# Column-tiled float32 numerators and denominators for all head pairs of a linear attention, and a lag of two units in the ELU layer behind it

## The chip, the core and the metric

The kernel runs on one core of a Trainium2 chip. Its engines are TensorE (PE in the profile; PEld is its weight load), VectorE (DVE), ScalarE (ACT), GpSimd (POOL) and SyncE (SP), which here only issues DMAs. Each engine works through its own instructions strictly in order; they wait for one another through semaphores. The metric is the device time of one launch in microseconds (us). A difference of under 0.5%, about 7 us, is taken as no change.

## The reference

```python
def phi(x):                                     # x: one head, 576 x 64
    proj = x @ w_phi                            # 128 features
    proj = proj - max(abs(proj), axis=-1)
    return concatenate([exp(proj), exp(-proj)]) # 256 features
q_p, k_p = phi(q), phi(k)                       # 4 batches x 8 heads
kv  = k_p.T @ v
num = q_p @ kv
den = q_p @ sum(k_p) + 1e-6
x   = num / den                                 # -> 2304 tokens x 512

x   = elu(x @ w_in) @ w_out                     # 512 -> 2048 -> 512
p   = domain_probs / sum(domain_probs)
out = sum over 4 experts of p[:, e] * (relu(x @ w1[e]) @ w2[e])   # 512 -> 1024 -> 512
```

All is float32.

## The kernel before, in words

**Stages.** Attention works on 16 pairs of heads; a pair fills 128 partitions (2 heads of 64). The ELU layer works on 9 token tiles of 256 tokens and, of its 2048 hidden features, on 4 units of 256 each for the first half (class `Elu`). The second half of the hidden features and the four experts follow in the classes `UpElu`, `Up`, `Out` and `Down`. Attention pairs 0 to 3 (the first batch) run alone, because every token tile needs all heads of a batch. Then the other pairs are fed in between the ELU products. In the same time the weights, which arrive as 64-bit floats, are converted by ScalarE, VectorE and GpSimd (`convert64`): 32 conversions for the first half of the hidden features, 32 for the second, whose VectorE work is held back (`hold`).

**Number forms.** Most products are done as three fp32r products of split operands, high x high, high x low and low x high, so an operand exists as `...h` and `...l`. Plain float32 products, which TensorE does in two passes (two matmul records each), are used in attention's projections, its keys-values product, and in the numerators of pairs 0 to 6 (`wide`, below `NF32`).

**One pair** (`pair`, a generator that yields between its steps). Projections (L192, each head on 64 of the array's 128 rows) -> `guard` on VectorE (L198, L199) -> exponentials of the keys (L202, L203) -> keys times values (L231, L232) into `kvw` (L280); queries transposed (L238) and their exponentials `ew` (L251), or `eh` and `el` (L256, L261) in the split form. The values' tile has columns of ones beside the 64 columns of values, so one product of 128 columns gives numerators in one half of the partitions and the denominator, repeated, in the other. `num` (L303) does that for each half of the 576 tokens: 4 float32 products, or 12 split ones, into two PSUM banks, copied to `nd` by ScalarE (L313). One row of `nd` goes by DMA to `dn`, laid out over 128 partitions (L320), VectorE adds 1e-6 and inverts (L323, L324), SyncE stores the reciprocals to DRAM (`rec`, L325) and loads them back broadcast over 64 partitions (`rb`, L329). VectorE multiplies (L334, once for each head), and `put_x` makes the high part on ScalarE (L295) and the low part on GpSimd (L298).

**One ELU unit** (`Elu`). `l1`: 24 products (L499 to L501) into one bank, then ScalarE (L507, L508), VectorE (L510), ScalarE's `gh` (L511) and `gl` (L512, VectorE or GpSimd). `l2`: 24 products with `gh` and `gl` (L528 to L530) into the tile's two accumulator banks. `drive` calls `l1` of a unit and then `l2` of the unit `LAG` before it. Between them `slot` advances attention (RATE steps a slot) and the weights (WRATE, WSLOW or WFAST steps).

**What sets the order.** The code gives each engine's instructions in the order of its loops; a scheduler then moves instructions on each engine by its own estimate of time and by priorities. In the first stage two steps of the weights' generator follow each step of attention (PRE). The pool for `gh` and `gl` has LAG + 1 buffers.

## Time and profile before

| | us |
|---|---|
| three timed runs, median | 1417.93 |
| lowest and highest | 1412.84, 1418.87 |
| the profiled execution | 1418.54 |
| its span, first to last instruction | 1416.7 |
| TensorE matmul busy in it | 1367.7 |
| VectorE, ScalarE, GpSimd busy | 692.8, 629.8, 418.6 |

The profile is of one execution. A line of its groups gives the source line, the engine, the operation, output<-inputs with shapes, the count, the busy time and mean of one, and then the idle time of the engine just before those instructions with what ended most of it. A matmul's modelled duration includes its way through the array, so consecutive matmuls overlap; how fast they follow one another is read from their start times. A row of the table of stretches has, for each engine, the busy time and the number of instructions, then the granted share of TensorE's 2.4 GHz clock.

### The profile page before, as it was taken

How to read it: one execution, taken by the hardware profiler on the slowest of the kernel's cores; microseconds unless marked ns; L12 is line 12 of the kernel's file. 1: busy time of each engine (PE TensorE's matmuls, PEld its weight loads, DVE VectorE, ACT ScalarE, POOL GpSimd, SP SyncE). 2: the span in 40 equal slices, each digit the busy share in tenths (PEclk: the TensorE clock that was granted, in tenths of full speed). 3: DMA queues.
4: the chain of work that ended last, by engine and by line, in shares of the span. 5: the costliest groups of instructions: out<-in, count | busy, mean ns of one | idle time of the engine just before them, and what ended most of it. 6: DMA issues, size and time to landing. Idle time of an engine off the chain costs nothing.

```text
span 1416.7 us, 21809 instructions
## 1 busy us (share of the span) xinstructions
PE 1367.7 (97%) x8224; PEld 1262.2 (89%) x8224; DVE 692.8 (49%) x1233; ACT 629.8 (44%) x1417; POOL 418.6 (30%) x487
## 2 busy tenths in 40 slices
PE   6779999999999999999999999999999999999998
PEld 5669999999989899999898979888898989889897
DVE  6786566666564566684423423224433325323232
ACT  6676676666556646573333442122431214321121
POOL 5567465454446211263202440002420004300000
PEclk9999999999999999999999999999999999999999
DMA  5453343433323230346425143434146351433521
GB/s 176 137 159 118 115 147 94 131 114 112 103 82 127 56 118 29 127 164 208 148 98 205 38 137 109 156 111 149 50 145 210 102 178 46 141 119 127 179 67 67
DMA packets 105786, 173.46 MB, mean 122 GB/s; under 512 B 33488, under 2 KB 51024, under 8 KB 105680
## 3 DMA queue, kind: packets, MB, share of 16 engines
q1 hardware_dynamic: 98224, 162.55, 35.3%
q10 hardware_dynamic: 7456, 9.52, 1.9%
q8 instruction: 65, 1.06, 0.3%
q14 instruction: 41, 0.34, 0.1%
HBM read 118.13 MB, written 53.81 MB: 121 GB/s over the span
## 4 chain that ended last, share of the span: by engine, by line
PE 75%; DMA 7%; issue 4%; DVE 4%; POOL 4%; ACT 3%; SPq 1%; ACTq 0%; DVEq 0%; POOLq 0%
PE bank L619 10%; PE bank L620 10%; PE bank L621 10%; PE bank L721 9%; PE bank L722 9%; PE bank L723 9%; PE bank L698 2%; PE bank L699 2%; PE bank L700 2%; PE bank L231 2%; PE bank L311 2%; PE bank L528 1%; PE bank L499 1%; PE bank L529 1%; PE bank L530 1%
## 5 line engine op out<-in xcount | busy, mean ns | idle before, releaser
L620 PE MATMUL bank<-xv,w 128*128 128x384 f32 x840 | 282.4, 336 | 0.0
L619 PE MATMUL bank<-xv,w 128*128 128x384 f32 x840 | 279.3, 337 | 2.5 <-DVE c L670 1.9
L621 PE MATMUL bank<-xv,w 128*128 128x384 f32 x840 | 278.2, 336 | 0.0
L721 PE MATMUL bank<-w,h 128*128 128x512 f32 x576 | 226.3, 396 | 2.3 <-ACT h L635 2.3
L722 PE MATMUL bank<-w,h 128*128 128x512 f32 x576 | 228.0, 396 | 0.0
L723 PE MATMUL bank<-w,h 128*128 128x512 f32 x576 | 202.8, 396 | 0.0
L461 POOL TENSOR_TENSOR w<-wst,w 128x256 fp32r<-128x256 f32 x100 | 78.0, 798 | 363.1 <-ACT w L460 220.4
L619 PEld LDWEIGHTS bank<-xv,w 128*128 128x128 f32 x840 | 158.2, 188 | 11.0 <-DVE c L670 2.2
L620 PEld LDWEIGHTS bank<-xv,w 128*128 128x128 f32 x840 | 158.3, 188 | 4.8
L621 PEld LDWEIGHTS bank<-xv,w 128*128 128x128 f32 x840 | 157.8, 188 | 0.0
L636 DVE SCALAR_TENSOR_TENSOR h<-bank,h 128x384 fp32r<-128x384 f32 x144 | 77.2, 554 | 125.9 <-ACT h L635 125.9
L635 ACT ACTIVATE h<-bank 128x384 fp32r<-128x384 f32 x144 | 66.8, 489 | 151.7 <-PE bank L621 95.4
L721 PEld LDWEIGHTS bank<-w,h 128*128 128x128 f32 x576 | 108.4, 188 | 25.4 <-ACT h L635 3.3
L722 PEld LDWEIGHTS bank<-w,h 128*128 128x128 f32 x576 | 108.5, 188 | 23.1
L723 PEld LDWEIGHTS bank<-w,h 128*128 128x128 f32 x576 | 107.2, 188 | 21.8 <-DVE h L636 1.0
L625 ACT ACTIVATE cmab<-bank 128x384 f32<-128x384 f32 x60 | 29.4, 491 | 192.5 <-PE bank L621 192.5
L570 POOL TENSOR_TENSOR xv<-xs,xv 128x768 fp32r<-128x768 f32 x24 | 47.7, 1988 | 190.3 <-ACT xv L569 181.5
L528 PE MATMUL bank<-gh,w 128*128 128x256 f32 x288 | 82.6, 295 | 6.7 <-ACT gh L511 6.7
L633 DVE TENSOR_TENSOR c<-cmab,bank 128x384 f32<-128x384 f32 x48 | 26.6, 554 | 120.3 <-ACT cmab L625 120.3
L499 PE MATMUL bank<-xh,w 128*128 128x256 f32 x288 | 83.8, 292 | 1.6 <-ACT eh L256 1.6
L633 DVE TENSOR_TENSOR bank<-cm,bank 128x384 f32<-128x384 f32 x48 | 26.9, 561 | 116.6 <-PE bank L621 101.1
L529 PE MATMUL bank<-gl,w 128*128 128x256 f32 x288 | 81.0, 283 | 1.7 <-DVE gl L512 1.7
(117 smaller groups left out, 2840.5 us busy)
## 6 DMA issues: line engine op xcount, KB each, us to landing
xv<-xvd SPq DMA_DIRECT2D x42, 768.0 KB, 4.4
wst<-in_w SPq DMA_DIRECT2D x64, 256.0 KB, 2.8
xvd<-xv SPq DMA_DIRECT2D x21, 768.0 KB, 4.0
yscr<-y SPq DMA_DIRECT2D x54, 256.0 KB, 2.2
y<-yscr SPq DMA_DIRECT2D x54, 256.0 KB, 3.2
w<-in_w_in SPq DMA_DIRECT2D x32, 256.0 KB, 3.4
w<-in_w_out SPq DMA_DIRECT2D x32, 256.0 KB, 3.3
kq<-in_kq SPq DMA_DIRECT2D x16, 320.0 KB, 3.6
```

Of the source, the lines that this page charges most:

```text
L461: on[WL[v % len(WL)]].tensor_tensor(out=lo, in0=x, in1=f32(hi), op=ALU.subtract)
L499: PE.matmul(ph[:, j], w[:, 0, c], xh[:, kc], start=(kc == 0), stop=False)
L528: PE.matmul(o, w[:, 0, c], self.gh[:, j], start=start, stop=False)
L529: PE.matmul(o, w[:, 0, c], self.gl[:, j], start=False, stop=False)
L619: PE.matmul(o, hi[:, c], x[:, 0, kc], start=not more and kc == 0, stop=False, skip_group_check=more)
L620: PE.matmul(o, hi[:, c], x[:, 1, kc], start=False, stop=False, skip_group_check=more)
L621: PE.matmul(o, lo[:, c], x[:, 0, kc], start=False, stop=kc == 1, skip_group_check=more)
L635: A.activation(h[:, 0], c, ACTF.Relu)
L636: V.scalar_tensor_tensor(out=h[:, 1], in0=c, scalar=0.0, in1=f32(h[:, 0]), op0=ALU.max, op1=ALU.subtract)
L721: PE.matmul(self.acc, h[:, 0, c], w[:, 0], start=f == 0, stop=False)
L722: PE.matmul(self.acc, h[:, 0, c], w[:, 1], start=False, stop=False)
L723: PE.matmul(self.acc, h[:, 1, c], w[:, 0], start=False, stop=f == 2 * NQ - 1)
```

## The change

All 16 pairs take the plain float32 form; the split form and its tiles go. The numerators of a pair's two heads are computed as products of 64 columns each (the stationary operand is only the 64 columns of values), head 0 to partitions 0 to 63 and head 1 to partitions 64 to 127 of one bank. The denominators come from products of their own, of 32 columns of ones each: four groups of 32 partitions hold the two heads and the two halves of the tokens. These are computed first, copied to `dd`, and sent to `dn` by one DMA of four rows. The pair has one step (one `yield`) less. The copy to `nd` is one for each half, and the multiplication is one over 128 partitions. `LAG` goes from 1 to 2.

```diff
-LAG = 1
+LAG = 2
...
-        def split(ef, c0, n):
-            for h in range(0 if wide else 2):
-                G.tensor_tensor(out=el[:, h, :, c0:c0 + n], in0=ef[:, h], in1=f32(eh[:, h, :, c0:c0 + n]), op=ALU.subtract)
...
-        A.activation(kvw if wide else kvh, pk, ACTF.Copy)
-        yield
-        if not wide:
-            V.tensor_tensor(out=kvl, in0=pk, in1=f32(kvh), op=ALU.subtract)
-        split(ef1, 256, 256)
-        split(efm, 512, D)
+        A.activation(kvw, pk, ACTF.Copy)
         yield
...
-        nd = [a1.tile([P, S], F32, tag=f"nd{h}", name=f"nd{h}", bufs=2) for h in range(2)]
+        nd = a1.tile([P, S], F32, tag="nd", name="nd", bufs=2)
...
         def num(s):
-            sl = slice(s * HS, (s + 1) * HS)
-            pn = [bank() for _ in range(2)]
-            terms = ((kvw, ew),) if wide else ((kvh, eh), (kvh, el), (kvl, eh))
-            last = 2 * len(terms) - 1
-            for h in range(2):
-                for k in range(last + 1):
-                    c, (w, m) = k // len(terms), terms[k % len(terms)]
-                    PE.matmul(pn[h][:, :HS], w[:, 2 * h + c], m[:, h, c, sl], start=(k == 0), stop=(k == last))
-            for h in range(2):
-                A.activation(nd[h][:, sl], pn[h][:, :HS], ACTF.Copy)
-
+            pn = bank()
+            for c in range(2):
+                for h in range(2):
+                    r = slice(h * D, h * D + D)
+                    PE.matmul(pn[r, :HS], kvw[:, 2 * h + c, r], ew[:, h, c, half(s)], start=(c == 0), stop=(c == 1))
+            A.activation(nd[:, half(s)], pn[:, :HS], ACTF.Copy)
+
+        def den():
+            pd = bank()
+            for c in range(2):
+                for h in range(2):
+                    for s in range(2):
+                        g = (2 * h + s) * Q
+                        ones = D - h * D
+                        PE.matmul(pd[g:g + Q, :HS], kvw[:, 2 * h + c, ones:ones + Q], ew[:, h, c, half(s)], start=(c == 0), stop=(c == 1))
+            A.activation(dd, pd[:, :HS], ACTF.Copy)
+
+        dd = a1.tile([P, HS], F32, tag="dd", name="dd")
+        den()
+        dn = a1.tile([P, S // D], F32, tag="dn", name="dn")
+        A.dma_start(dn, dd[::Q].rearrange("g (a b) -> g a b", b=S // D))
+        yield
         num(0)
-        yield
         num(1)
-        dn = a1.tile([P, S // D], F32, tag="dn", name="dn")
-        for h in range(2):
-            A.dma_start(dn[h * D:h * D + D], nd[h][D - h * D:D - h * D + 1, :].rearrange("o (a b) -> o a b", b=S // D))
         yield
...
-        for h in range(2):
-            r = slice(h * D, h * D + D)
-            with tc.issue_after(mark[0]):
-                V.tensor_tensor(out=xf[r], in0=nd[h][r], in1=rb[r], op=ALU.mult)
+        with tc.issue_after(mark[0]):
+            V.tensor_tensor(out=xf, in0=nd, in1=rb, op=ALU.mult)
```

The changed file is 19 lines shorter, so a line such as L499 is L480 in it. In the order of instructions, products that the code issues are counted, so a float32 product is one row and two records of the trace.

TensorE in the first stage, from the keys-values products of the second pair to the first transpose of the third. Before:

```order
L232 MATMUL bank<-vt_186,kpm 128x128
L192 MATMUL bank<-wbd,kq 128x128 x8
L311 MATMUL bank<-ew,kvw 128x288 x4
L192 MATMUL bank<-wbd,kq 128x128 x8
L311 MATMUL bank<-ew,kvw 128x288 x4
L238 MATMUL bank<-ident,qd_496 128x128
```

and now (L294 is `den`, L284 is `num`, L190 the projections):

```order
L230 MATMUL bank<-vt_186,kpm 128x128
L190 MATMUL bank<-wbd,kq 128x128 x8
L294 MATMUL bank<-ew,kvw 32x288 x8
L284 MATMUL bank<-ew,kvw 64x288 x8
L190 MATMUL bank<-wbd,kq 128x128 x8
L236 MATMUL bank<-ident,qd_504 128x128
```

The last numerators stood behind the second group of projections; now denominators and numerators stand ahead of it.

TensorE among the ELU products, at the numerators of the sixth pair. Before:

```order
L500 MATMUL bank<-xl,w 128x256
L501 MATMUL bank<-xh,w 128x256
L311 MATMUL bank<-ew,kvw 128x288 x4
L499 MATMUL bank<-xh,w 128x256
L500 MATMUL bank<-xl,w 128x256
```

and now, at the denominators of the same pair (L480 to L482 are the first layer's products, L509 to L511 the second layer's):

```order
L481 MATMUL bank<-xl,w 128x256
L482 MATMUL bank<-xh,w 128x256
L294 MATMUL bank<-ew,kvw 32x288 x8
L509 MATMUL bank<-gh,w 128x256
L510 MATMUL bank<-gl,w 128x256
L511 MATMUL bank<-gh,w 128x256
```

Untiled products had untiled ones on both sides; the denominators, and 12 rows later the numerators, are tiled ones among untiled.

TensorE at a change from the first to the second layer's products, after attention has ended. Before:

```order
L501 MATMUL bank<-xh,w 128x256
L528 MATMUL bank<-gh,w 128x256 x2
L499 MATMUL bank<-xh,w 128x256
L500 MATMUL bank<-xl,w 128x256
L501 MATMUL bank<-xh,w 128x256
L529 MATMUL bank<-gl,w 128x256
L530 MATMUL bank<-gh,w 128x256
L528 MATMUL bank<-gh,w 128x256
```

and now:

```order
L480 MATMUL bank<-xh,w 128x256
L481 MATMUL bank<-xl,w 128x256
L482 MATMUL bank<-xh,w 128x256
L509 MATMUL bank<-gh,w 128x256
L510 MATMUL bank<-gl,w 128x256
L511 MATMUL bank<-gh,w 128x256
```

The scheduler had put first-layer products between the two that need `gh` alone and the first that needs `gl`; now 24 and 24 stand in plain blocks.

## Rows read from the trace of the kernel before

**Rows 1.** The page's first part: busy time, share of the span, instructions.

```profile
PE 1367.7 (97%) x8224; PEld 1262.2 (89%) x8224; DVE 692.8 (49%) x1233; ACT 629.8 (44%) x1417; POOL 418.6 (30%) x487
```

**Rows 2.** Busy time in stretches: stretch, length, each engine, clock, DMA share, GB/s.

```profile
0.00:88.80 88.80, 64.77 (x502) 55.76 (x502) 65.79 (x150) 57.70 (x153) 48.69 (x77) 0.96 0.53 155
88.80:106.30 17.50, 11.84 (x82) 10.20 (x80) 14.94 (x30) 12.89 (x34) 11.12 (x17) 1.00 0.53 166
106.30:386.00 279.70, 276.75 (x2290) 266.49 (x2290) 176.53 (x348) 181.41 (x436) 151.82 (x191) 0.99 0.38 114
...
473.00:1416.70 943.70, 933.67 (x4747) 851.44 (x4746) 389.46 (x645) 328.63 (x701) 164.96 (x164) 1.00 0.36 122
...
107.00:111.00 4.00, 4.00 (x24) 4.00 (x23) 3.25 (x7) 3.31 (x8) 3.43 (x5) 0.57 0.01 4
```

**Rows 3.** TensorE's groups of the ELU products, and one piece of its timeline.

```profile
L499 PE MATMUL bank<-xh,w 128*128 128x256 f32 x288 | 83.8, 292 | 1.6 <-ACT eh L256 1.6
L528 PE MATMUL bank<-gh,w 128*128 128x256 f32 x288 | 82.6, 295 | 6.7 <-ACT gh L511 6.7
L529 PE MATMUL bank<-gl,w 128*128 128x256 f32 x288 | 81.0, 283 | 1.7 <-DVE gl L512 1.7
...
106.34 0.50 PE L528 MATMUL bank<-gh,w 128*128 128x256 f32 x2 [3.91 <-ACT gh L511]
```

**Rows 4.** Timeline of TensorE at one half's wide numerators: start, us, what.

```profile
125.42 2.10 PE L311 MATMUL bank<-ew,kvw 128*128 128x288 f32 x8
127.15 0.50 PE L499 MATMUL bank<-xh,w 128*128 128x256 f32 x1
127.48 0.28 PE L500 MATMUL bank<-xl,w 128*128 128x256 f32 x1
```

**Rows 5.** Timeline of TensorE at one half's split numerators, first record and next line.

```profile
219.94 0.29 PE L311 MATMUL bank<-eh,kvh 128*128 128x288 f32 x1
...
221.53 0.28 PE L528 MATMUL bank<-gh,w 128*128 128x256 f32 x1
```

**Rows 6.** Timeline of TensorE: full height, a start of half height, a whole visit.

```profile
20.75 1.06 PE L231 MATMUL bank<-vt,kp 128*128 128x128 f32 x8
...
23.07 0.38 PE L192 MATMUL bank<-wbd,kq 64*128 64x128 f32 x2
...
146.34 0.28 PE L530 MATMUL bank<-gh,w 128*128 128x256 f32 x1
146.55 1.16 PE L192 MATMUL bank<-wbd,kq 64*128 64x128 f32 x16
147.64 0.39 PE L528 MATMUL bank<-gh,w 128*128 128x256 f32 x1
147.87 0.28 PE L529 MATMUL bank<-gl,w 128*128 128x256 f32 x1
```

**Rows 7.** The start up to 107 us: GpSimd, VectorE's groups, waits, SyncE's timeline.

```profile
97.98 1.75 POOL L298 TENSOR_TENSOR xl<-xf,xh 128x256 fp32r<-128x256 f32 x3
...
L334 DVE TENSOR_TENSOR xf<-nd,rb 64x576 f32<-64x576 f32 x8 | 7.4, 919 | 0.1
L116 DVE TENSOR_SCALAR pcs<-pcs 128x256 f32<-128x256 f32 x26 | 11.2, 430 | 11.6 <-ACT pcs L112 11.5
...
SPq L325 <- DMA dn<-nd: 15.2, 4, 8.1
...
59.98 0.42 SPq L148 DMA_DIRECT2D kq<-in_kq  x1
69.31 0.33 SPq L325 DMA_DIRECT2D rec<-dn  x1
```

**Rows 8.** Timeline of VectorE and TensorE at the end of the ELU layer.

```profile
469.79 0.42 DVE L448 TENSOR_TENSOR wtmp<-wst 128x256 f32<-128x256 f32 x1
...
469.93 0.69 PE L619 MATMUL bank<-xv,w 128*128 128x384 f32 x1 [1.90 <-DVE c L670]
```

More of the change, by code (lines that the diff above doesn't have):

```diff
@@ L23 @@
 HS = S // 2
+Q = 32
 TS = 256
@@ L55 @@
 PB = 4
-NF32 = 7
 LDB = 1
@@ L183, in pair @@
         kt, qt = kq[:, :512], kq[:, 640:]
-        wide = i < NF32
         def proj(src):
@@ L239, in tpose @@
             return pt
-        if wide:
-            ew = a1.tile([P, 2, 2, S], F32, tag=("eh", "el")[i % 2], name="ew")
-        else:
-            eh = a1.tile([P, 2, 2, S], F32R, tag="eh", name="eh")
-            el = a1.tile([P, 2, 2, S], F32R, tag="el", name="el")
+        ew = a1.tile([P, 2, 2, S], F32, tag=("eh", "el")[i % 2], name="ew")
         def qexp(ps, c0, n):
             src = ps[:, :512].rearrange("p (h s) -> p h s", h=2)[:, :, :n] if n > P else blocks(ps, 2)[:, :, P - n:]
-            if wide:
-                for c, sc in ((0, 1.0), (1, -1.0)):
-                    A.activation(ew[:, :, c, c0:c0 + n], src, ACTF.Exp, scale=sc)
-                return None
-            ef = a1.tile([P, 2, 2, n], F32, tag=f"ef{n}", name="ef")
-            for dst in (ef, eh[:, :, :, c0:c0 + n]):
-                for c, sc in ((0, 1.0), (1, -1.0)):
-                    A.activation(dst[:, :, c], src, ACTF.Exp, scale=sc)
-            return ef
-        def split(ef, c0, n):
-            for h in range(0 if wide else 2):
-                G.tensor_tensor(out=el[:, h, :, c0:c0 + n], in0=ef[:, h], in1=f32(eh[:, h, :, c0:c0 + n]), op=ALU.subtract)
-        if wide:
-            kvw = a1.tile([P, 4, P], F32, tag=("kvh", "kvl")[i % 2], name="kvw")
-        else:
-            kvh = a1.tile([P, 4, P], F32R, tag="kvh", name="kvh")
-            kvl = a1.tile([P, 4, P], F32R, tag="kvl", name="kvl")
-        ef0 = qexp(tpose(0), 0, 256)
+            for c, sc in ((0, 1.0), (1, -1.0)):
+                A.activation(ew[:, :, c, c0:c0 + n], src, ACTF.Exp, scale=sc)
+        kvw = a1.tile([P, 4, P], F32, tag=("kvh", "kvl")[i % 2], name="kvw")
+        qexp(tpose(0), 0, 256)
         kv(0, 0)
@@ L271, in pair @@
         yield
-        split(ef0, 0, 256)
-        ef1 = qexp(tpose(1), 256, 256)
+        qexp(tpose(1), 256, 256)
         pt = bank()
@@ L276, in pair @@
             PE.transpose(pt[:, h * P:(h + 1) * P], md[:, h], ident)
-        efm = qexp(pt, 512, D)
+        qexp(pt, 512, D)
         kv(1, 0)
         kv(1, 1)
-        A.activation(kvw if wide else kvh, pk, ACTF.Copy)
-        yield
-        if not wide:
-            V.tensor_tensor(out=kvl, in0=pk, in1=f32(kvh), op=ALU.subtract)
-        split(ef1, 256, 256)
-        split(efm, 512, D)
+        A.activation(kvw, pk, ACTF.Copy)
         yield
@@ L299, in put_x, with half @@
                 o += n
-        nd = [a1.tile([P, S], F32, tag=f"nd{h}", name=f"nd{h}", bufs=2) for h in range(2)]
+        nd = a1.tile([P, S], F32, tag="nd", name="nd", bufs=2)
+        def half(s):
+            return slice(s * HS, (s + 1) * HS)
         def num(s):
-            sl = slice(s * HS, (s + 1) * HS)
-            pn = [bank() for _ in range(2)]
-            terms = ((kvw, ew),) if wide else ((kvh, eh), (kvh, el), (kvl, eh))
-            last = 2 * len(terms) - 1
-            for h in range(2):
-                for k in range(last + 1):
-                    c, (w, m) = k // len(terms), terms[k % len(terms)]
-                    PE.matmul(pn[h][:, :HS], w[:, 2 * h + c], m[:, h, c, sl], start=(k == 0), stop=(k == last))
-            for h in range(2):
-                A.activation(nd[h][:, sl], pn[h][:, :HS], ACTF.Copy)
+            pn = bank()
[18 more added lines that the diff above has]
+        yield
         num(0)
-        yield
         num(1)
-        dn = a1.tile([P, S // D], F32, tag="dn", name="dn")
-        for h in range(2):
-            A.dma_start(dn[h * D:h * D + D], nd[h][D - h * D:D - h * D + 1, :].rearrange("o (a b) -> o a b", b=S // D))
         yield
```

## The prediction

> **What bounds the kernel now.** I read the busy line first, then the table of stretches, then TensorE's waits, and then single pieces of its timeline. The busy line [rows 1] has TensorE's matmuls at 97% of the span and no other engine at 50%. The table of stretches [rows 2] shows where the rest is. Until 88.8 us, four head pairs go through attention alone and TensorE is busy 64.77 us of it. Until 106.3 us the ELU layer starts up, 11.84 of 17.5 us busy. From 106.3 to 386 us attention and the ELU layer run side by side and TensorE is busy 276.75 of 279.70 us. In the two layers after 473 us it is busy 933.67 of 943.70 us. So from 106.3 us on the time is TensorE's own work plus its few waits. An instruction taken from ScalarE, VectorE or GpSimd there is worth only the wait that it ends. Before 106.3 us it is the other way round: TensorE waits for those engines and for DMAs.
>
> The profiled execution took 1418.54 us, its span 1416.7 us, and the median of the three timed runs is 1417.93 us. I make the sum as a difference and add it to the median.
>
> **Part 1, the numerators on TensorE.** Every float32 product of the code has two matmul records. The eight records of one half in the wide form start at 125.42 us [rows 4]. The second record after them starts at 127.48 us, one usual step of 0.12 us late. That makes 1.94 us for eight, 0.243 us each. A wide pair has 16 of them, 3.88 us. In the split form twelve records run from 219.94 to 221.53 us [rows 5], 0.1325 us each. A split pair has 24, 3.18 us. So the plain form costs TensorE more, not less. In the saturated stretch stand the numerators of 12 pairs, 4 to 15: three wide and nine split, 3 x 3.88 + 9 x 3.18 = 40.3 us.
>
> The new form has 16 records of 64 columns for the numerators and 16 of 32 columns for the denominators, each still with 288 moving columns, so I leave each at 0.243 us. If tiles of other columns run at once, the numerators take 8 turns and the denominators 4: 12 x 0.243 = 2.91 us a pair, 34.9 us in all. If they take turns it is 32 x 0.243 = 7.76 us, 93.1 us in all. The trace of before has no column tile. The nearest row is the row tile of the projections [rows 6]: eight records at full height and 128 moving columns take 1.06 us, the last one 0.28 us of it, so 0.111 us a step. Sixteen records at half height take 1.16 us, and without the last one's 0.27 us that is 0.89 us, 0.056 us a step. Two tiles ran fully at once. I take 34.9 us, a gain of 5.4 us, and keep 93.1 us as the far end.
>
> Each change of tiling costs something too. From the L530 at 146.34 us over 16 half-height records to the L529 at 147.87 us are 1.53 us [rows 6]. The records take 8 x 0.111 = 0.89 us of it and two usual steps 0.24 us, so going in and coming out cost 0.39 us, 0.195 us a change. In the order of instructions from the first ELU product on there are 57 such changes before and 97 now, because denominators and numerators of a pair stand apart among ELU products. 40 x 0.195 = 7.8 us, lost. With smaller weights a change may cost half of that, 3.9 us; it can't be below nothing. Part 1 together: -5.4 + 7.8 = +2.4 us.
>
> The Trainium skill ("TensorE: Matmul & The Clock Gate", Part 3, measured speedup against the span model) gives three column tiles of 32 columns with 512 moving columns as 2.38 times as fast as one after the other, not three times. By that the 34.9 us would be an estimated 44.0 us, 9.1 us more; no run here shows column tiles yet.
>
> **Part 2, the lag of two.** The waits that it is about stand at L528 and L529, for ScalarE's gh and VectorE's gl: 6.7 and 1.7 us in the whole span [rows 3]. One of 3.91 us, at 106.34 us, belongs to the start (part 3). The other 4.5 us lie mostly after 386 us, where attention no longer fills in. With a lag of two another unit's 24 products, 24 x 0.12 = 2.9 us, lie between a unit's first and second layer. The order shows plain blocks of 24 and 24 there. All 4.5 us go, and nothing is late next, since the same two operands are the last to come. L499's 1.6 us behind ScalarE's eh [rows 3] go with the split form, whose twelve activations a pair become six. Together -6.1 us. At least the 1.6 us could come back as another in-order wait on ScalarE, so I keep -4.5 as the near end. The other freed ScalarE and GpSimd time is worth nothing: TensorE is busy there.
>
> **Part 3, the start.** The first second-layer product at 106.34 us [rows 3] marks saturation. In the new order TensorE has more to do once the fourth pair's x is there: 63 first-layer products (7.6 us), one pair's denominators and numerators (2.9 us), a projection (0.9 us) and six changes (1.2 us), 12.6 us. Before, all of that but the third unit's 24 products (2.9 us) was done by 106.3 us. So it breaks even if x is ready at 106.3 - 9.7 = 96.6 us. GpSimd ended x at 97.98 + 1.75 = 99.7 us [rows 7].
>
> What moves that point? On VectorE four multiplications of 0.919 us go, because one over 128 partitions replaces two over 64: -3.7 us. But 26 weight conversions now stand ahead of it in the order, not 22: four of each of four operations of about 0.42 us, as the row of L116 [rows 7], +6.8 us. Against these stand waits that can shrink. SyncE's queue stood 15.2 us, in four stretches of up to 8.1 us, at the store of the reciprocals, waiting for the denominators' DMA [rows 7]; between 60.4 and 69.31 us it issued nothing, with the next weights and values queued behind. So ScalarE had no new weights to convert and VectorE waited 11.5 us for ScalarE's pcs. Now the denominators are computed ahead of the numerators and ahead of the next projection, and their DMA leaves that much earlier. If no wait is saved, x is 3.1 us later (102.8). If all 11.5 us are saved it is 8.4 us earlier (91.3). I take half, 97.0 us, so +0.4 us. The ends are -5.3 and +6.2 us.
>
> The clock fell to its lower level (1.2 of 2.4 GHz) for most of 107 to 111 us, 0.57 granted on average [rows 2], after the wait of 3.91 us. The new order waits for x instead, so I expect one such fall again and change nothing for it.
>
> **Part 4, the end of the ELU layer.** TensorE waited 1.90 us at 469.93 us for VectorE's c, which stood behind two weight operations [rows 8]. In the new order a third stands ahead of it: 0.42 us, +0.4 us. The last 72 second-layer products instead of 48 only swap places with first-layer ones. From 473 us on the products are the same.
>
> **Sum.** +2.4 - 6.1 + 0.4 + 0.4 = -2.9 us, so 1415 us.
>
> **Rivals.** *A, column tiles take turns.* TensorE gets 93.1 us in place of 34.9 us, +58.2 us: 1473 us. For it: every numerator tile reads all 128 partitions again, while the half-height tiles of [rows 6] shared one read of 128. Against it: those tiles did run at once in float32. It decides early: the sum has 2.9 us in hand, and with the 7.1 us that make a measurable difference, 10 of the 58 us, a sixth of the overlap, are enough to make the kernel slower.
>
> *B, the overlap is partial.* If the two records of a float32 product must follow each other before the next tile's first may start, denominators run two at a time, not four: 4 x 0.243 x 12 = +11.7 us, 1427 us. Against it: at 23.07 us two records of different tiles started within 0.02 us [rows 6], so the second did not wait for the first product's other pass.
>
> The Trainium skill (the same page, Part 3, what overlaps and what doesn't) says that matmuls start and end strictly in program order. By that B is the rule if the two records are neighbours in the program; the row of 23.07 us doesn't settle how they are issued. Its 2.38 of three would end in the same place, an estimated 1424 us.
>
> *C, the start shrinks further.* All of VectorE's wait goes (-5.3 in place of +0.4) and a change of tiling costs half: 1415 - 5.7 - 3.9 = 1405 us. For it: the queue stood 15.2 us. Against it: four more conversions.
>
> **Chances.** The forecast 0.52, with its own range 1410 to 1422; C 0.24; B 0.10; A 0.14. A measurement of this kernel can't tell less than 0.5% (7.1 us) from no change. Faster by more is C and little else, 0.25. Within are the forecast but for its edges and some of B, 0.53. Slower are A and most of B, 0.22. The range goes from a little under C, 1402, to a little above B, 1432, and leaves out A and some edges.
>
> **What would show it.** Part 1: in the new profile the line of the numerators should show eight records of 64 columns in about 1.2 us, and eight products of 32 columns (16 records) in about 1.2 us too; 2 us for eight or 4 us for 16 mean A. Part 2: no wait at the second layer's products after 386 us. Part 3: the first of them at about 109 us with 72 first-layer products done; SyncE's wait at the store of the reciprocals well under 15 us. Part 4: the wait near 470 us stays. I am wrong if the stretch that was 106.3 to 453 us grows or shrinks by over 8 us, or if the last layers change at all.

## The result, and the profile after

The changed kernel takes 1422.55 us (median of 10 runs, 1418.54 to 1430.36), the kernel before 1416.34 us (10 runs). The ratio is 1.0053, 95% interval 1.0035 to 1.0070: slower by half a per cent, where I had forecast 1415 us. The interval lies on both sides of the half per cent that is taken as no change. The profiled execution of the changed kernel took 1427.12 us, 8.6 us above that of before.

The busy line of the page has the same shape as in [rows 1]:

```profile
PE 1369.6 (96%) x8408; PEld 1242.8 (87%) x8408; DVE 664.5 (47%) x1208; ACT 603.7 (42%) x1347; POOL 362.6 (25%) x433
```

TensorE is busy 1.9 us longer in a span that is 8.6 us longer, so most of the loss is waiting. To find its place I cut each span at four events that every kernel here has: the first product of the first layer, the last of the second layer, the product behind the first hundred of L600 (the next layer's products), the end. The table of stretches of the kernel before (stretch, length, busy time of PE, PEld, DVE, ACT, POOL, granted clock, DMA share, GB/s):

```profile
0.00:88.82 88.82, 64.79 (x503) 55.77 (x503) 65.81 (x150) 57.72 (x153) 48.71 (x77) 0.96 0.53 155
88.82:454.89 366.07, 353.61 (x2900) 340.38 (x2898) 231.46 (x429) 232.57 (x544) 194.95 (x240) 1.00 0.38 115
454.89:554.28 99.39, 96.80 (x544) 95.62 (x542) 57.40 (x94) 57.58 (x117) 19.37 (x13) 0.98 0.25 79
554.28:1416.70 862.42, 852.49 (x4285) 770.48 (x4284) 338.17 (x561) 281.90 (x607) 155.61 (x159) 1.00 0.37 127
```

and of the changed kernel:

```profile
0.00:101.12 101.12, 67.52 (x550) 56.94 (x551) 73.39 (x172) 63.30 (x166) 58.51 (x92) 0.86 0.52 155
101.12:463.53 362.41, 353.62 (x3037) 319.35 (x3035) 195.97 (x382) 200.40 (x460) 129.02 (x170) 0.99 0.36 110
463.53:567.63 104.10, 98.26 (x543) 97.27 (x542) 57.90 (x94) 57.89 (x117) 19.70 (x13) 0.97 0.26 80
567.63:1425.30 857.67, 850.25 (x4285) 769.18 (x4284) 337.19 (x561) 282.08 (x607) 155.32 (x159) 1.00 0.37 128
```

The start is 12.3 us longer, at a granted clock of 0.86 instead of 0.96. The ELU layer is 3.7 us shorter, the passage to the next layer 4.7 us longer, and the rest 4.8 us shorter. The last is chance of one execution: in all the other profiles of this study the rest took 857 to 859 us, and only this one of before had a wait of 2.07 us and then half clock for 3.4 us, at 848 us.

Chance is in the other stages too. Two kernels of the next section, "drains first" and "other bank", have the changed kernel's work in the same order on TensorE, VectorE, ScalarE and GpSimd up to the end of the ELU layer. Their layers took 356.7 and 357.0 us, not 362.4 us; this is the layer of "other bank":

```profile
101.15:458.11 356.96, 348.15 (x3037) 315.37 (x3035) 196.29 (x382) 200.01 (x460) 129.41 (x170) 1.00 0.37 112
```

In the start four kernels share one order (these three and "lag of one"), and took 99.0 to 101.2 us. So against before the start is 10 to 12 us longer and the layer 4 to 9 us shorter.

What the change was to do on TensorE, it did. TensorE's timeline of the changed kernel around one pair's denominators (L294) and numerators (L284):

```profile
155.99 0.28 PE L482 MATMUL bank<-xh,w 128*128 128x256 f32 x1
156.19 1.18 PE L294 MATMUL bank<-ew,kvw 128*32 128x288 f32 x16
157.30 0.39 PE L509 MATMUL bank<-gh,w 128*128 128x256 f32 x1
...
158.72 0.28 PE L511 MATMUL bank<-gh,w 128*128 128x256 f32 x1
158.93 2.16 PE L284 MATMUL bank<-ew,kvw 128*64 128x288 f32 x16
161.02 0.38 PE L509 MATMUL bank<-gh,w 128*128 128x256 f32 x1
161.25 0.28 PE L510 MATMUL bank<-gl,w 128*128 128x256 f32 x1
```

Sixteen records of 32 columns take 1.18 us and sixteen of 64 columns 2.16 us. With a step of 0.243 us [rows 4], four and eight turns are 0.97 and 1.94 us; the rest is mostly the time that the last record lasts beyond its step. So the column tiles run fully at once. The first tiled record starts 0.21 us behind the last full product instead of a usual step of 0.12 us; coming out, the next product is 0.1 us late and the one behind it 0.1 us too. Reckoned as from [rows 6], the two visits cost 0.33 and 0.35 us, 0.17 us a change, a little under the 0.195 us taken there.

The waits for gh and gl [rows 3] are gone. The page's groups of the second layer:

```profile
L509 PE MATMUL bank<-gh,w 128*128 128x256 f32 x288 | 84.3, 293 | 0.0
...
L510 PE MATMUL bank<-gl,w 128*128 128x256 f32 x288 | 81.2, 282 | 0.2 <-DVE gl L493 0.2
```

Now the start. TensorE's timeline in one turn of the pair loop, from one first query transpose (L236) to the next:

```profile
34.66 0.45 PE L236 MATMUL bank<-ident,qd 128*128 128x128 f32 x1 [4.71 <-ACT w L128]
34.90 1.92 PE L229 MATMUL bank<-vt,kp 128*128 128x128 f32 x8
...
45.57 1.18 PE L294 MATMUL bank<-ew,kvw 128*32 128x288 f32 x16 [1.07 <-ACT kvw L258]
46.68 2.16 PE L284 MATMUL bank<-ew,kvw 128*64 128x288 f32 x16
48.77 1.16 PE L190 MATMUL bank<-wbd,kq 64*128 64x128 f32 x16
54.24 0.45 PE L236 MATMUL bank<-ident,qd 128*128 128x128 f32 x1 [4.31 <-DVE dn L306]
```

Denominators and numerators, 3.2 us together, stand ahead of the next pair's query projection (L190, 48.77 us). Behind the projection TensorE has nothing, and waits 4.31 us until VectorE has guarded the queries (the rows name the instruction beside that guard in the queue). Before, one half of the numerators stood ahead of the projection and the other behind it. The same wait was 4.71, 4.57 and 3.89 us in the turns around it (before, 0.38 to 3.28 us), and at the end of each of the four the granted clock was at half (1.2 of 2.4 GHz) for 3.4 or 6.8 us. Eight records that take 1.06 us at full clock [rows 6] take 1.92 us at 34.90 us. The stretch of the changed kernel there:

```profile
33.20:40.00 6.80, 5.34 (x23) 5.11 (x24) 4.85 (x13) 2.98 (x8) 3.31 (x6) 0.50 0.30 82
```

VectorE's timeline in the end of the same turn, and then ScalarE's:

```profile
51.08 0.43 DVE L116 TENSOR_SCALAR pcs<-pcs 128x256 f32<-128x256 f32 x1 [1.70 <-ACT pcs L112]
...
51.89 0.68 DVE L196 TENSOR_REDUCE mx<-bank 128x4 f32<-128x512 f32 x1
...
53.41 0.68 DVE L197 TENSOR_TENSOR qd<-bank,mx 128x512 f32<-128x512 f32 x1
```

```profile
49.84 0.39 ACT L285 ACTIVATE nd<-bank 128x288 f32<-128x288 f32 x1
50.13 0.62 ACT L200 ACTIVATE kp<-kp 128x512 f32<-128x512 f32 x1
50.65 0.39 ACT L112 ACTIVATE pcs<-w 128x256 f32<-128x256 f32 x1
```

The queries are projected by 49.9 us, but the guard (L196) starts at 51.89 us: a weight conversion stands ahead of it in VectorE's queue and waits for ScalarE's L112, which stands behind the copy of the numerators (L285) and an exponential of the keys (L200). That ScalarE was late is not the copy's doing alone: it had stood 0.76 us at a weight's DMA just before, at 48.62 us. Between the first five pairs' transposes 6, 6, 4 and 6 conversions end on VectorE; before it was 6, 3, 4 and 4. So two things are mixed: the numerators' place, and the conversions' number.

At the end of the ELU layer, ScalarE's timeline (L453 converts weights, L523 drains the layer's sums):

```profile
465.26 0.63 ACT L453 ACTIVATE w<-wst 128x512 fp32r<-128x512 f32 x1 [2.21 <-DMA wst<-wout]
465.79 0.58 ACT L523 ACTIVATE xs<-bank 128x512 f32<-128x512 f32 x1
...
466.79 0.59 ACT L523 ACTIVATE xs<-bank 128x512 f32<-128x512 f32 x1
```

TensorE's first product of the next layer (an "up" product, L600) waits for the last of these drains. I take it that it was given the PSUM bank which this drain reads ("other bank" below tries that); before, it started at 455.01 us, ahead of the last drain at 455.55 us, so its bank was another. Now:

```profile
467.43 0.69 PE L600 MATMUL bank<-xv,w 128*128 128x384 f32 x1 [3.63 <-ACT xs L523]
```

### The profile page after: what moved, and what is told of

It reads as the page before. It is cut to its first block, busy times and chain, and to the rows that moved or that the text cites. A ratio compares the mean times of both kernels' runs of the same rounds, so it can differ in the third digit from the quotient of the medians.

```text
span 1425.3 us, 22008 instructions
## 1 busy us (share of the span) xinstructions
PE 1369.6 (96%) x8408; PEld 1242.8 (87%) x8408; DVE 664.5 (47%) x1208; ACT 603.7 (42%) x1347; POOL 362.6 (25%) x433
## 4 chain that ended last, share of the span: by engine, by line
PE 76%; DMA 7%; DVE 4%; issue 3%; ACT 3%; POOL 2%; SPq 1%; ACTq 0%; DVEq 0%; POOLq 0%
PE bank L600 10%; PE bank L602 10%; PE bank L601 10%; PE bank L702 9%; PE bank L703 9%; PE bank L704 9%; PE bank L679 2%; PE bank L680 2%; PE bank L681 2%; PE bank L229 2%; PE bank L480 2%; PE bank L284 1%; PE bank L509 1%; PE bank L482 1%; PE bank L481 1%
## 5 line engine op out<-in xcount | busy, mean ns | idle before, releaser
L600 PE MATMUL bank<-xv,w 128*128 128x384 f32 x840 | 279.7, 337 | 5.8 <-ACT xs L523 3.6
L442 POOL TENSOR_TENSOR w<-wst,w 128x256 fp32r<-128x256 f32 x100 | 78.7, 806 | 366.6 <-ACT w L441 357.0
L600 PEld LDWEIGHTS bank<-xv,w 128*128 128x128 f32 x840 | 158.6, 189 | 14.3 <-ACT xs L523 3.8
L480 PE MATMUL bank<-xh,w 128*128 128x256 f32 x288 | 85.6, 297 | 2.0 <-ACT xh L268 1.9
L509 PE MATMUL bank<-gh,w 128*128 128x256 f32 x288 | 84.3, 293 | 0.0
L481 PE MATMUL bank<-xl,w 128*128 128x256 f32 x288 | 82.8, 288 | 0.0
L482 PE MATMUL bank<-xh,w 128*128 128x256 f32 x288 | 82.8, 287 | 0.0
L510 PE MATMUL bank<-gl,w 128*128 128x256 f32 x288 | 81.2, 282 | 0.2 <-DVE gl L493 0.2
```

Of the source, the lines that this page charges most:

```text
L442: on[WL[v % len(WL)]].tensor_tensor(out=lo, in0=x, in1=f32(hi), op=ALU.subtract)
L480: PE.matmul(ph[:, j], w[:, 0, c], xh[:, kc], start=(kc == 0), stop=False)
L481: PE.matmul(ph[:, j], w[:, 0, c], xl[:, kc], start=False, stop=False)
L482: PE.matmul(ph[:, j], w[:, 1, c], xh[:, kc], start=False, stop=(kc == KD - 1))
L509: PE.matmul(o, w[:, 0, c], self.gh[:, j], start=start, stop=False)
L510: PE.matmul(o, w[:, 0, c], self.gl[:, j], start=False, stop=False)
```

## The experiments

The kernels can be told apart by the lengths of their stages in their profiles (us; "turn" is the mean of the first four turns of the pair loop, "conversions" those that end on VectorE in each, "start", "ELU layer" and "passage" the first three stretches above) and by the median of their 4 to 12 runs:

| kernel | median | ratio to before | turn | conversions | start | ELU layer | passage |
|---|---|---|---|---|---|---|---|
| before | 1416.3 | | 16.6 | 6,3,4,4 | 88.8 | 366.1 | 99.4 |
| changed | 1422.6 | 1.0035 to 1.0070 | 19.2 | 6,6,4,6 | 101.1 | 362.4 | 104.1 |
| lag of one | 1415.9 | 0.9986 to 1.0007 | 18.9 | 6,6,4,6 | 99.0 | 358.2 | 100.2 |
| drains first | 1422.0 | 1.0018 to 1.0051 | 18.8 | 6,6,4,6 | 99.4 | 356.7 | 102.2 |
| other bank | 1421.6 | 1.0020 to 1.0051 | 19.2 | 6,6,4,6 | 101.2 | 357.0 | 103.3 |
| filler | 1411.3 | 0.9940 to 0.9973 | 18.4 | 6,4,4,4 | 95.9 | 354.3 | 101.6 |
| four conversions | 1412.9 | 0.9955 to 0.9991 | 17.8 | 5,4,4,4 | 95.0 | 354.8 | 102.8 |
| late numerators | 1393.5 | 0.9822 to 0.9853 | 15.5 | 5,4,4,4 | 83.9 | 346.4 | 102.3 |
| late, lag of one | 1397.8 | 0.9843 to 0.9876 | 16.1 | 5,4,4,4 | 87.1 | 354.3 | 99.8 |
| late denominators too | 1396.8 | 0.9832 to 0.9877 | 15.8 | 5,4,4,4 | 87.9 | 346.0 | 102.3 |
| late, three conversions | 1399.4 | 0.9851 to 0.9896 | 15.1 | 4,3,3,3 | 82.4 | 357.2 | 101.3 |
| before, late | 1405.9 | 0.9906 to 0.9934 | 16.7 | 5,4,4,4 | 89.4 | 356.9 | 100.9 |
| untiled, late | 1407.0 | 0.9908 to 0.9938 | 16.5 | 5,4,4,4 | 90.3 | 353.9 | 102.2 |

The lengths are of one execution each. Kernels with one and the same order differed by up to 3.2 us in the start ("late numerators" 83.9 us, "late, lag of one" 87.1 us) and by 5.7 us in the layer, so smaller differences there say nothing.

**Late numerators.** Both halves go one step later, behind the next pair's query projection.

```diff
         yield
+        yield
         num(0)
         num(1)
-        yield
         with tc.issue_after(mark[0]):
```

> The changed kernel with the column-tiled numerators put one step later, behind the next pair's query projection; the denominators stay ahead of it. Theory T: in the start the query projection of the next pair comes some 2 us earlier in each turn, TensorE has 2.2 us of numerators to do while VectorE prepares the queries, its waits there fall from 4.3 to 4.7 us to 2 to 3 us, the clock does not fall between 30 and 95 us, a turn takes 16 to 17 us instead of 18.5 to 20, the first product of the first layer comes at 87 to 92 us instead of 101, and the sum is 1410 to 1415 us. Rival R1 (more weight conversions ahead of the first layer, VectorE being the bound of the start): a turn stays at 19 us or more, the sum within 2 us of 1422. Rival R3 (tiling changes): no change in a turn, since it has the same tiled products and one more change of tiling, 1422 to 1425 us.

1393.49 us (1391.91 to 1397.26): 29 us below the changed kernel, 23 us below before, more than twice the gain that I expected of it. TensorE's timeline in the same turn as above:

```profile
41.79 2.15 PE L294 MATMUL bank<-ew,kvw 128*32 128x288 f32 x16 [3.00 <-ACT kvw L258]
43.87 1.70 PE L190 MATMUL bank<-wbd,kq 64*128 64x128 f32 x16
45.50 2.16 PE L284 MATMUL bank<-ew,kvw 128*64 128x288 f32 x16
48.14 0.30 PE L236 MATMUL bank<-ident,qd 128*128 128x128 f32 x1 [0.48 <-DVE qd L197]
```

From the denominators to the next transposes are 6.35 us instead of 8.67 us (45.57 to 54.24), and the wait of 4.31 us is 0.48 us. The clock fell here too, at 41.6 and 58.7 us, for 3.4 us each (the first is why the denominators take 2.15 us); I had expected no fall. What I had not expected either is the second stretch. The stages of this kernel:

```profile
0.00:83.86 83.86, 62.58 (x550) 51.20 (x551) 63.85 (x151) 58.26 (x151) 49.78 (x79) 0.90 0.56 168
83.86:430.24 346.38, 345.48 (x3037) 313.94 (x3036) 208.80 (x402) 206.78 (x475) 140.54 (x184) 1.00 0.40 120
```

In the ELU layer TensorE is idle 0.9 us of 346.38 us; in the changed kernel it was 8.8 us of 362.41 us, and its 3037 records were busy 8.1 us longer. About 5 us of these 8.1 are clock: half clock of 6.8 us at 203.9 us and of 3.4 us at 326.7 us, behind waits of 1.88 and 1.57 us; the late kernel has none there. But "other bank", with the changed kernel's order, has none there either and is busy 348.15 us. Set beside it, the layer is 10.6 us shorter and not 16 us; 7.9 us of that are waits.

**Four conversions.** TensorE's order stays that of the changed kernel; VectorE may have only four conversions in a turn. `n` counts the conversions, and `gq` holds each pair's last query guard, behind which the next four are held. (The file is longer: L196, L202, L203, L243 and L291 are the L190, L196, L197, L236 and L284 of the changed kernel.)

```diff
+        k = (n - 3) // 4
+        while len(gq) <= k and done[0] < NP:
+            yield
+        after = mark[0] if hold else gq[k] if 0 <= k < len(gq) else None
-        with tc.issue_after(mark[0]) if hold else nullcontext():
+        with tc.issue_after(after) if after is not None else nullcontext():
             V.tensor_scalar(out=ps, ...)
...
         guard(qd[1], pq1, 4)
+        gq.append(mark[0])
```

> The changed kernel with TensorE's order as it is (denominators and numerators ahead of the next query projection), but no more than four weight conversions standing on VectorE in each turn of the start, where the changed kernel has 6, 6, 4 and 6 and the kernel before 6, 3, 4 and 4. It separates two readings that the late numerators left mixed, since with them the conversions of a turn fell to four as well. Rival R1 (the conversions that the order puts between a turn's operations are the loss): a turn of 16 to 17 us, the first product of the first layer at 86 to 92 us, 1408 to 1414 us. Theory T (the numerators ahead of the query projection are the loss, with the clock that falls behind the long wait): a turn stays at 18 us or more, the waits of TensorE for the guarded queries at 3.5 us or more, the first layer starts at 96 to 101 us, 1417 to 1424 us.

1412.92 us (1407.11 to 1419.04), a turn of 17.8 us, start 95.0 us. The time is in R1's range, while the turn and the start lie between the two readings, so each has a part. VectorE's timeline, where it now waits, and TensorE's:

```profile
44.42 1.27 DVE L203 TENSOR_TENSOR kp<-bank,mx 128x512 f32<-128x512 f32 x2
48.67 1.29 DVE L202 TENSOR_REDUCE mx<-bank 128x4 f32<-128x512 f32 x2 [2.98 <-PE bank L196]
49.87 0.68 DVE L203 TENSOR_TENSOR qd<-bank,mx 128x512 f32<-128x512 f32 x1
```

```profile
45.38 2.16 PE L291 MATMUL bank<-ew,kvw 128*64 128x288 f32 x16
47.48 1.16 PE L196 MATMUL bank<-wbd,kq 64*128 64x128 f32 x16
50.70 0.30 PE L243 MATMUL bank<-ident,qd 128*128 128x128 f32 x1 [2.06 <-DVE dn L313]
```

With fewer conversions VectorE is free at 45.7 us and waits 2.98 us for the query projection, which stands behind 2.16 us of numerators. That is the numerators' part. Fewer conversions took 19.2 - 17.8 = 1.4 us off a turn; the late numerators, at the same number of conversions, another 2.2 us. The kernel before has 17 conversions in the four turns, as this one has, and its turn is still 17.8 - 16.6 = 1.2 us shorter. So the 2.6 us by which the change lengthened a turn are some 1.4 us of conversions and some 1.2 us of the new order on TensorE, with the clock in both. (This edit also moves the conversions behind the guards, so it is not their number alone.)

**Filler.** The numerators of the first four pairs are computed a second time behind the projection, to no use but to keep TensorE busy.

```diff
         num(0)
         num(1)
         yield
+        if i < NP:
+            num(0, False)
+            num(1, False)
```

> The changed kernel, with the numerators of the first four pairs computed a second time behind the next pair's query projection; the second results are not used, the output stays the same. It fills 2.2 us of TensorE's idle time in each of four turns and moves nothing else. If the clock's falls (theory T) are most of the loss: waits split into less than 2.5 us, no half clock between 30 and 90 us, a turn of 17 to 17.8 us, first product of the first layer at 93 to 96 us, 1414 to 1418 us. If the later query projection alone is the loss (the other half of T): turns stay at 19 us, 1421 to 1424 us. Rival R1 (VectorE and conversions): turns stay at 19 us.

1411.29 us (1408.34 to 1413.85): four times 2.16 us of TensorE's work more, and 11 us less time, a time below all the readings. TensorE's waits for the guarded queries shrank to 0.2 to 2.3 us, and yet the turn is 18.4 us. But it is no clean test of the clock. The scheduler, which places VectorE's work by its own reckoning of times, now put four conversions in three of the four turns, and the clock still fell at the wait for kvw (3.2 us, at 45.4 us). The clock's own share stays open.

**Lag of one**, in the changed kernel and in the late one.

```diff
-LAG = 2
+LAG = 1
```

> The changed kernel with a lag of one unit instead of two, all else as changed. Theory T (the start's order and clock cost some 12 us, the lag saves in the ELU layer and costs at its end): first product of the first layer still near 101 us, since the lag is not used there; waits of 4 to 7 us on the ELU units come back before the second layer's products; the 3.6 us wait of the first up product on the last drains goes, with half of the 6.8 us at half clock behind it; the sum stays near the changed kernel, 1420 to 1427 us. Rival R2 (the lag itself is what costs): 1415 to 1418 us, the start too being quicker. Rival R3 (the column tiling costs, by its tiling changes): as T, near 1422 us, but with the 12 us lost wherever tiled products stand.

> The changed kernel with late numerators and a lag of one unit. Theory (a lag of two saves the waits for the ELU units): waits of 3 to 7 us in front of the second layer's products come back, 1396.5 to 1400 us. Rival R2 (a lag of two is worth nothing, or costs at the end of the layer): 1389 to 1395 us.

In the changed kernel a lag of one is 6.7 us faster (1415.87 us), against the theory and in the range of R2: with it, the rest of the change takes as long as the kernel before (0.9986 to 1.0007). In the late kernel it is 4.3 us slower (1397.75 us). TensorE's waits in the ELU layer of the late one with a lag of one (us in total, times, longest), where the late kernel with two has 0.8 us in all (this profile is of the slowest of its four runs, 1400.88 us):

```profile
PE bank L294 <- ACT kvw L258: 1.8, 3, 0.9
PE bank L510 <- DVE gl L493: 1.3, 2, 0.9
PE bank L190 <- DVE md L197: 1.1, 1, 1.1
PE bank L509 <- ACT gh L492: 0.9, 2, 0.5
```

Only L509's and L510's, 2.2 us, are the waits for gh and gl that the lag is about; I had expected 3 to 7 us. The passage is 2.5 us (late) and 3.9 us (changed) shorter with a lag of one. So in the late kernel the lag of two saves waits in the layer and pays some 3 us at its end. What it costs in the changed kernel is not settled: the passage has 2 to 4 us of the 6.7 us, and the layers, 358.2 us with a lag of one against 356.7, 357.0 and 362.4 us in three executions with two, don't show the rest.

**Drains first.** ScalarE's first w2 conversions are held behind the last drain.

```diff
+                with tc.issue_after(drained[0]):
                     A.activation(w[:, 0], t, ACTF.Copy)
```

> The changed kernel with ScalarE's conversions of the first w2 weights issued behind the last drain of the ELU layer, instead of ahead of it. Theory T: the first up product no longer waits 3.6 us at 467 us, the wait is under 1 us, the 6.8 us at half clock behind it shrink to 3.4 us or less, and the sum is 3 to 6 us below the changed kernel, 1416.5 to 1419.5 us; the start stays (first product of the first layer near 101 us). Rival (the wait is handed on to the w2 weights, which come later): a wait of 2 us or more at the first partial sums, and 1421 to 1424 us.

1422.03 us: no gain, and the first up product still waits 2.7 us for the drains. ScalarE's timeline (L527 is the drain, L523 in the changed kernel):

```profile
456.87 0.60 ACT L527 ACTIVATE xs<-bank 128x512 f32<-128x512 f32 x1 [2.42 <-DMA x1scr<-xs]
...
458.41 0.60 ACT L527 ACTIVATE xs<-bank 128x512 f32<-128x512 f32 x1 [0.94 <-DMA x1scr<-xs]
```

The drain has two buffers, and with a lag of two the products of the last four drains end within 3.6 us (in the changed kernel 460.21 to 463.81 us) instead of 5.0 us (before, 450.17 to 455.17 us): the third waits for the first one's store.

**Other bank.** The first up product gets a bank that is free.

```diff
     psum[0] = pool("psum2", 8, space=PSUM)
+    for _ in range(2):
+        V.memset(bank()[:, :16], 0.0)
     ups[0].begin()
```

> The changed kernel; the order of TensorE's instructions is the same, but two small writes of VectorE hold the PSUM banks 0 and 1 while the first up product is given its bank, so that it takes bank 6, which the accumulator of the last tile but one has left, instead of bank 0, which the very last drain of the ELU layer has yet to read. Theory (the 3.6 us wait at 467 us is a matter of which bank comes first): the wait is under 0.5 us, the half clock behind it 3.4 us or less, 1417 to 1419.5 us. Rival (the drains hold something else too, or VectorE's first sums wait behind the two writes): a wait of 2 us or more in the next 10 us, 1421 to 1424 us.

1421.57 us: the rival was right. The wait is gone, and comes back in four pieces in the next 21 us (TensorE's timeline, with the two longest):

```profile
458.23 0.33 PE L600 MATMUL bank<-xv,w 128*128 128x384 f32 x1
...
467.58 0.44 PE L600 MATMUL bank<-xv,w 128*128 128x384 f32 x1 [1.89 <-ACT cm L606]
...
478.75 0.45 PE L600 MATMUL bank<-xv,w 128*128 128x384 f32 x1 [1.93 <-DVE c L651]
```

The late kernel starts its up products without a wait too, and its passage takes 102.3 us. So the loss in the passage is not this bank's, or hardly: 103.3 us in place of 104.1 us.

**Before, late**: the kernel before with both halves of its numerators behind the projection. **Untiled, late**: the same with plain float32 for all pairs and a lag of two, without column tiles.

```diff
-        num(0)
         yield
+        num(0)
         num(1)
```

```diff
-LAG = 1
+LAG = 2
...
-NF32 = 7
+NF32 = 16
```

> The kernel before with nothing changed but the place of the numerators' first half: one step later, behind the next pair's query projection, with the second half. If what counts is that nothing long stands ahead of the query projection (theory T), the kernel before gains as well: the turn in the start shrinks by up to 2 us, the first product of the first layer comes at 82 to 86 us instead of 88.8, and the sum is 1402 to 1411 us. Rival (the place matters only to the changed kernel, because before had a second half there to fill the wait): within 3 us of 1416, and waits of about 2 us shorter in one place and longer in another.

> The kernel before with plain float32 numerators for all pairs, each product over all 128 columns (no column tiles, no separate denominators), a lag of two units, and both halves of the numerators behind the next pair's query projection. Set beside the changed kernel with late numerators (1393.5 us) it prices the column tiling: 3.88 us a pair instead of 2.91, that is 1.0 us for each of the 11 pairs whose numerators stand in the full stretch (and nothing in the start, where TensorE waits), less the tiling changes that it does not have, up to 7.8 us. Theory (tiles are worth their difference): 1397 to 1404 us. Rival R3 (tiling changes eat it): 1390 to 1396 us.

The kernel before gains 11 us by the order alone (1405.87 us), but not where I said: its turn stays at 16.7 us and the ELU layer is 9.2 us shorter. TensorE's two projections of a pair now stand as one visit (ten changes of tiling fewer from the first ELU product on), and its idle time in the layer falls from 12.5 to 7.9 us; the other half of the 9.2 us I can't account for. So in the order of before it made no difference to the turn that 2.2 us of numerators stood ahead of the projection. Plain numerators for all pairs and the lag then add 1.1 us (1406.96 us), which is within the spread of the runs (1404.8 to 1409.2 us). The column tiles with their separate denominators take 13.5 us off that (1393.49 us), more than either range that I had given allows.

**Late denominators too** and **late, three conversions**: is there more to gain in the start?

```diff
+        yield
+        yield
         den()
...
-        yield
         num(0)
         num(1)
```

> The changed kernel with denominators and numerators both behind the next pair's query projection, so that nothing that waits for the exponentiated keys' products stands ahead of it; the chain of the reciprocals starts some 2 us later in a turn for it. Theory T: the waits of 3.0, 2.1 and 1.4 us in front of the denominators no longer hold up the query projection; a turn of 14.5 to 16 us (VectorE has some 13 us of work in it), the first product of the first layer at 80 to 84 us, 1388 to 1394 us. Rival (the later reciprocals make x late, and x of the fourth pair is what starts the layer): the first layer at 84 to 88 us or a wait of 2 us or more there, 1394 to 1399 us.

```diff
-        k = (n - 3) // 4
+        k = (n - 3) // 3
```

> The changed kernel with late numerators (1393.5 us) and at most three weight conversions on VectorE in each turn of the start, where that kernel had four. If VectorE's load still sets the turn there (four conversions of some 1.7 us and 6 us of guards in 15.5 us): a turn of 14 to 15 us, the first product of the first layer at 79 to 82 us; the conversions left out stand in the first units of the ELU layer, whose products may wait 1 to 3 us for them; 1388 to 1393 us. If the chain from the keys' products over the numerators to the queries sets the turn: turns stay at 15.5 us and the later conversions cost, 1394 to 1399 us.

The first took 1396.76 us: hardly anything waits for kvw any more, but TensorE waits 1.8 to 3.8 us a turn for the guarded queries, and x of the fourth pair ends at 95.2 us instead of 88.1 us: the rival. The second (on top of the late numerators; its output is not the reference's, probably because conversions that are held overwrite each other's scratch, while its instructions are of the same number and kind, so only its times are used) has three turns of 13.7 to 14.1 us, and one of 18.6 us with half clock in it. With one conversion less, four operations of about 0.42 us, those turns are some 1.6 us shorter: VectorE's load has a part in the turn here too. But the ELU layer, in which the conversions left out must be done, takes 357.2 us instead of 346.4 us, and the sum is 1399.35 us.

## Why the prediction was wrong

The time lies inside my range of 1402 to 1432 us, but on the far side of before, and that it lies inside is luck. I had given the slower outcome to A and B, and neither happened; nor did C, a shorter start.

**Part 1** was right in its mechanism and short in what it is worth. Column tiles run fully at once; the changes of tiling cost 0.17 us each, near the 0.195 us taken. Rivals A and B are out. The Trainium skill ("TensorE: Matmul & The Clock Gate", Part 3, measured speedup against the span model) gives 2.38 for three column tiles of 32 columns and 512 moving columns. That case was not run; here four tiles with 288 moving columns took four turns for 16 records, 0.97 us, a quarter of 16 times 0.243 us, and for this kernel the measurement decides. What I had wrong is that I counted only the 12 pairs in the full stretch and put nothing on the start. Set beside the untiled kernel, a turn there is 16.50 - 15.51 = 0.99 us shorter, about the 0.97 us by which a pair's numerators became shorter, though single turns of one kernel differ by over 2 us. By my own terms the tiles are worth 12 x 0.97 = 11.6 us less 54 more changes at 0.195 us, 10.5 us: -1.1 us. In the late order they are worth -13.5 us; the profiles have 6.4 us of it in the start and 7.5 us in the ELU layer, of that 4.3 us waits. Of the 6.4 us some 3 us can be chance, by the starts of 83.9 and 87.1 us above.

**Part 2** was right in its mechanism: no wait of note is left at the second layer's products. Its size holds only in the late order, where the lag of two measured -4.3 us, after some 2.5 us lost in the passage; I had -4.5 us. In the changed kernel itself the same lag measured +6.7 us, and the cause is open beyond the passage. The 1.6 us behind ScalarE's eh came back, as my near end allowed: L480 waits 1.9 us for ScalarE's xh.

**Part 3 is the step that failed most.** I wrote that "the denominators are computed ahead of the numerators and ahead of the next projection, and their DMA leaves that much earlier", and took x of the fourth pair to be ready at 97.0 us. GpSimd ended it in the changed kernel at

```profile
103.37 1.02 POOL L271 TENSOR_TENSOR xl<-xf,xh 128x256 fp32r<-128x256 f32 x2
```

that is at 104.4 us, 4.7 us later than before [rows 7] and beyond the upper end that I had (102.8 us). The term that failed is the half of VectorE's 11.5 us of waits that I took as saved. The denominators' DMA no longer holds up the store of the reciprocals, but the store now waits for VectorE, 14.1 us in all in place of 15.2 us, and VectorE's wait for pcs grew to 18.4 us (waits up to 107 us: total, times, longest):

```profile
DVE pcs L116 <- ACT pcs L112: 18.4, 15, 2.7
SPq L308 <- DVE pcs L117: 12.9, 3, 4.6
```

The price of the four further conversions, +6.8 us, was about right: with the conversions held to four in a turn the start is 6.1 us shorter. And I saw that the projection was pushed back and put no price on it, as if the start were a sum of loads. It is a ring: projection, guard, transposes, keys' products, kvw, projection. Between kvw and the next projection stand 3.2 us now and stood 2.2 us before; behind the projection the other 2.2 us of numerators had been filling TensorE's wait, and nothing fills it now. Moving the numerators there took 2.2 us off a turn at an equal number of conversions. That this place alone sets the turn is not shown: "before, late" gained nothing in its turn. The clock I counted with one fall; there were four between 33 and 98 us, 20 us at half clock, and before had none there.

**Part 4** was too small. The wait near 470 us became 1.64 us, at 486.5 us, but a new one of 3.63 us came ahead of it, and the passage grew by 4.7 us: 3.4 us more of waits, and half clock for 6.8 us instead of 3.4 us. I had said that the last 72 products "only swap places"; with the lag of two the drains also fall due closer together, and even "other bank", without that wait, has a passage of 103.3 us.

The ELU layer itself came out at -3.7 us, which is what Parts 1 and 2 add up to. That is luck. The prediction counted from the first product of the second layer and gave the wait of 3.91 us ahead of it to the start. That product came at 115.97 us instead of 106.34 us, with 24 more first-layer products (2.9 us) and the same attention work done. Counted so, the start is 6.7 us longer, where I had +0.4 us (my own reckoning gives 104.4 - 96.6 = +7.8 us for x at 104.4 us, so it was x that I had wrong), and the layer behind it 1.9 us longer. In "drains first" and "other bank" it is 3.9 and 3.6 us shorter, so the forecast of the layer was near for the order, but not for its reasons: TensorE is idle 6.4 to 8.8 us in the layers of these three, mostly ahead of attention's products, which I had not foreseen, and 0.9 us with the numerators moved.

## What to carry to other kernels

Where several engines hand one item round in a ring, look first at what stands between the last result of a turn and the first instruction of the next, on the engine's own queue: here 2.2 us of work moved behind that instruction, with what the scheduler moved along, was worth 29 us. When work is moved, ask what it had been covering where it stood; here the wait that lost its filler grew from 0.4 to 3.3 us to 3.9 to 4.7 us a turn, with half clock at its end. And a scheduler that reckons times of its own moves other work as well, so count the other queues' instructions in each experiment before giving its gain to the edit. Last, profile one order more than once: here that moved a stage of 360 us by 5.7 us.

## What was not expected of the hardware

Two passes of float32 products on four column tiles did not hold each other up: at 156.19 us the four tiles' first records start within 0.02 us of each other. The granted clock of the changed kernel was at half behind waits of 1.57 to 4.71 us in the start and in the layer, six times. Its spread from run to run (12 us in 10 runs) is not explained by that alone: two of its runs with a mean granted clock of 0.987 took 1418.54 and 1429.83 us.
